# Two attention branches on one core: dense pieces that have no due date go into fewer and fuller slots

## The chip, the core and the metric

The kernel runs on one core of a Trainium2 chip. The metric is the device time in microseconds of one execution; three runs are given and their median is the time. Durations in the text come from one further execution that the hardware profiler recorded.

## The reference

Two attention branches over 2048 tokens of width 640 with 32 heads of 20, whose outputs stand side by side in the result. In short:

```python
# branch A: four segments of 512 tokens; q, k, v = x @ wq, wk, wv
for s in range(4):
    p = softmax(q[s] @ k[s].T * Dh**-0.5 + mask)      # mask falls on keys that come before the query
    a_mem = (phi(q[s]) @ M) / (phi(q[s]) @ z + 1e-6)    # phi(t) = t + 1 where t > 0, else exp(t)
    o[s] = g * a_mem + (1 - g) * (p @ v[s])             # g = sigmoid(beta), per head
    M = M + phi(k[s]).T @ v[s]; z = z + phi(k[s]).sum()
A = o @ wo
# branch B: q, k, v = x @ wqkv; causal window of 256 keys
B = softmax(where(0 <= i - j < 256, q @ k.T * Dh**-0.5, -1e9)) @ v @ wo
out = concatenate([A, B], axis=-1)
```

All arrays are bf16.

## The kernel before

The tokens are worked in four chunks of 512, and for each chunk the B branch and then the A branch: eight phases B0, A0, B1, A1, B2, A2, B3, A3. In a phase the 32 heads are eight groups of four (`Unit`). The scores of a group are cut into rectangles of key blocks and query blocks, and `Phase` puts them into packs of up to 512 query columns (`Pack`): 20 packs in a phase of A and in B0, 24 in the other phases of B, 172 in all.

Each pack is a **slot** of the loop in `body`, and slots are numbered through from 0 (B0 0 to 19, A0 20 to 39, B1 40 to 63, A1 64 to 83, B2 84 to 107, A2 108 to 127, B3 128 to 151, A3 152 to 171). The schedule is manual: what `body` records in this order is the order of each engine's queue. In one slot it does the following.

- It first runs what was put down for this slot (`self.after`): the spread of finished q or k from DRAM scratch into four row groups (L291, four DMAs on SP), and `normalise` (L544, L549 on DVE) of a group that was weighed four slots earlier (three in the last phase), which needs the transposed copy `ocT` that SP fetches by a DMA (L529).
- `scores` (L459) multiplies q and k on TensorE into two `Sc` tiles, one for two heads each. There are three such tiles in PSUM. ScalarE takes exp of each into `pt` (L465), and GpSimd clears what the masks exclude (L479, L485).
- It runs what was put down behind the scores (`self.behind`): for the memory of A, the phi of a projection made one and two slots before, an exp on ScalarE (L310) and steps on VectorE (L308, L313).
- Where a group's last pack lies two slots back, `weigh` (L514) multiplies its probabilities with v into a `D` tile; VectorE copies it (L527) and SP transposes it.
- Then come **dense pieces** that `pick` chooses: projections of q and k (`proj`, L267, copied at L270 and stored by L271), v for the coming chunk (`vproj`, L326, emptied at L332 or L334), and in A the memory's update (`upd`, L402) and read (`read`, L435, emptied by L442, L444 and L445), and halves of the output product (`out_half`, L580, emptied at L583, stored by L587).

Weighing and all dense pieces write PSUM tiles named `D`, of which there are two, so that a piece can start when VectorE has emptied the tile of the piece before the last one.

The planner of `body` has a cost for each piece in its own units: 1.19 for a projection, 0.79 for a v half, 0.75 for an output half and for a weighing, 0.4 for a read or an update, 0.45 for the scores. `total` is their sum over the phase, `part` the share of the phase's packs by weight that is done with this slot, and `room = total * part - done` is how far the phase lags behind an even spread. A piece may have a due slot; then `due` is what must be done now so that it isn't late, and where `due` is above `room` it takes its place and no output half is allowed. `pick` looks at the next three pieces of each kind and takes the combination whose cost comes nearest to `room`, with a term for the share of each kind that should be done by then.

Due dates stand on the pieces of B0, the first value and projection pieces of A0 and the first half of B1 (and on slot 13 of B1); the pieces of the later phases have none. What is left at a phase's end is done there, so that each phase has the same pieces in any case.

Of the kernel before, what the change touches and what calls it, by code (L numbers as in the profile page):

```python
# [82 lines left out]
class Kern:  # L83
# [572 lines left out]
    def body(self):  # L656
        phases = [Phase(br, c) for c in range(NC) for br in "BA"]
        lists, upd = self.plan()
        self.turned, self.half = [], []
        self.closing, self.open_masks = False, []  # L660
        for n, ph in enumerate(phases):
            dense = lists[n]
            mem = []
            if ph.br == "A" and ph.c > 0:
                mem = [(0.4, lambda tt=tt, hf=hf: self.read(ph.c, tt, hf))
                       for hf in range(2) for tt in range(CT)] + upd[ph.c]
            outs = 2 * OUT_TILES[n]
            np_ = len(ph.packs)
            weights = [pk.weight for pk in ph.packs]
            base = 0.45 * np_  # L670
            total = base + sum(a[0] for a in dense + mem) + 0.75 * outs + 0.75 * G
            done = 0.0
            at = [0, 0, 0]
            for i, pk in enumerate(ph.packs):
                while any(a[2] is not None and a[2] <= i for a in dense[at[0]:]):
                    done += dense[at[0]][0]
                    dense[at[0]][1]()
                    at[0] += 1
                for f in self.after.pop(self.slot, []):
                    f()  # L680
                last = n == len(phases) - 1 and i == np_ - 1
                if last:
                    self.last_turn("A", NC - 1, 0, 3)
                self.scores(pk, last)
                done += 0.45
                for f in self.behind.pop(self.slot, []):
                    f()
                if last:
                    break
                if self.ready and self.ready[0][0] <= self.slot:  # L690
                    self.weigh(self.ready.pop(0)[1])
                    done += 0.75
                self.prefetch()
                part = sum(weights[:i + 1]) / sum(weights)
                can = 2 * sum(1 for t in self.turned if t[0] + 2 <= self.slot) + len(self.half)
                room, ahead, due = total * part - done, 0.0, 0.0
                for a in dense[at[0]:]:
                    ahead += a[0]
                    if a[2] is not None:
                        due = max(due, ahead - 1.7 * (a[2] - 1 - i))  # L700
                if due > room:
                    room, can = due, 0
                for kind in self.pick(part, room, dense[at[0]:at[0] + 3],
                                      mem[at[1]:at[1] + 3], min(outs - at[2], can, 3),
                                      at, (len(dense), len(mem), outs)):
                    if kind == 2:
                        done += 0.75
                        self.out_step()
                    else:
                        a = (dense, mem)[kind][at[kind]]  # L710
                        done += a[0]
                        a[1]()
                    at[kind] += 1
                self.slot += 1
            for a in dense[at[0]:] + mem[at[1]:]:
                a[1]()
        self.tail("A", NC - 1)
# [101 lines left out]
```

## Time and profile before

| | us |
|---|---|
| median of 3 runs | 393.15 |
| lowest and highest run | 392.26, 395.36 |
| profiled execution | 390.19 |
| its span, from first to last instruction | 388.1 |
| TensorE matmul busy | 340.4 (88%) |
| ScalarE busy | 338.1 (87%) |
| VectorE busy | 276.7 (71%) |
| GpSimd busy | 251.8 (65%) |
| mean granted clock of TensorE | 0.991 of full speed |

PE in the profile is TensorE (matmuls; PEld is its weight load), ACT is ScalarE, DVE is VectorE, POOL is GpSimd and SP the engine that issues all DMAs of the kernel. Busy is the time in which an engine has at least one instruction in work. A row of the time order gives start, duration, engine, line, operation, tiles written and read, the number of instructions merged into it, and in square brackets how long the engine stood idle before it and who released it. A row of a stretch gives its bounds, its length, the busy time of each engine, the granted clock and the share of the DMA engines.

### The profile page before, as it was taken

How to read it: one execution, taken by the hardware profiler on the slowest of the kernel's cores; microseconds unless marked ns; L12 is line 12 of the kernel's file. 1: busy time of each engine (PE TensorE's matmuls, PEld its weight loads, DVE VectorE, ACT ScalarE, POOL GpSimd, SP SyncE). 2: the span in 40 equal slices, each digit the busy share in tenths (PEclk: the TensorE clock that was granted, in tenths of full speed). 3: DMA queues.
4: the chain of work that ended last, by engine and by line, in shares of the span. 5: the costliest groups of instructions: out<-in, count | busy, mean ns of one | idle time of the engine just before them, and what ended most of it. 6: DMA issues, size and time to landing. Idle time of an engine off the chain costs nothing.

```text
span 388.1 us, 10554 instructions
## 1 busy us (share of the span) xinstructions
PE 340.4 (88%) x4060; PEld 161.3 (42%) x4060; DVE 276.7 (71%) x581; ACT 338.1 (87%) x384; POOL 251.8 (65%) x392
## 2 busy tenths in 40 slices
PE   7999988977998798988997989898999989988884
PEld 3433434322443344444543335444454435544442
DVE  2467667634788868788778886789877887777583
ACT  2867789985999889888999999988999999999972
POOL 9657564542777587635578888844458988955550
PEclk9999999998999989999999999999999999999999
DMA  8993328647434597728575697758474377736312
GB/s 256 314 285 77 47 83 151 113 105 187 134 80 134 143 173 141 135 71 137 117 135 135 127 190 126 149 104 110 116 146 120 92 169 129 113 78 113 96 30 70
DMA packets 110738, 50.77 MB, mean 131 GB/s; under 512 B 81760, under 2 KB 110688, under 8 KB 110688
## 3 DMA queue, kind: packets, MB, share of 16 engines
q1 hardware_dynamic: 110688, 50.10, 61.1%
q8 instruction: 32, 0.52, 0.6%
q14 instruction: 18, 0.15, 0.1%
HBM read 16.39 MB, written 14.42 MB: 79 GB/s over the span
## 4 chain that ended last, share of the span: by engine, by line
PE 42%; ACT 24%; DVE 16%; issue 6%; POOL 6%; DMA 3%; SPq 0%; POOLq 0%; DVEq 0%; ACTq 0%
ACT pt L465 22%; PE D L267 13%; PE Sc L459 7%; PE D L326 6%; PE D L580 5%; PE D L514 5%; PE D L253 4%; POOL pt L479 3%; DVE qk L270 3%; POOL pt L485 3%; DVE oc L527 3%; ACT pe L310 2%; PE Sc L628 2%; DVE omem L445 1%; DMA ocT<-oc 1%
## 5 line engine op out<-in xcount | busy, mean ns | idle before, releaser
L465 ACT ACTIVATE pt<-Sc 128x1024 bf16<-128x1024 f32 (+1 forms) x344 | 320.7, 1077 | 32.3 <-PE Sc L459 28.2
L479 POOL TENSOR_SCALAR_AFFINE_SELECT pt<-pt 128x512 bf16<-128x512 bf16 x254 | 167.6, 671 | 117.2 <-ACT pt L465 116.9
L485 POOL TENSOR_SCALAR_AFFINE_SELECT pt<-pt 128x512 bf16<-128x512 bf16 x112 | 78.6, 717 | 5.1 <-ACT pt L465 4.8
L270 DVE CAST qk<-D 128x512 bf16<-128x512 f32 x70 | 47.9, 687 | 29.4 <-PE D L267 26.8
L527 DVE CAST oc<-D 128x512 bf16<-128x512 f32 x62 | 42.7, 688 | 19.9 <-PE D L514 19.8
L459 PE MATMUL Sc<-qpB,kpB 20*128 20x256 bf16 (+2 forms) x704 | 43.3, 277 | 7.8 <-ACT pt L465 4.7
L459 PE MATMUL Sc<-qpA,kpA 20*128 20x384 bf16 (+3 forms) x512 | 41.0, 302 | 5.8 <-ACT pt L465 5.0
L580 PEld LDWEIGHTS <-oT 128*128 128x128 bf16 x280 | 25.4, 98 | 17.9 <-issue 6.6
L583 DVE CAST ot<-D 128x320 bf16<-128x320 f32 x56 | 27.0, 485 | 7.2 <-PE D L580 6.4
L459 PEld LDWEIGHTS <-kpB 20*128 20x128 bf16 x704 | 13.6, 92 | 42.5 <-issue 38.5
L267 PE MATMUL D<-xTA,Aq 128*128 128x512 bf16 x100 | 24.9, 379 | 4.6 <-DVE oc L527 3.5
L326 PE MATMUL D<-Av,xTA 128*128 128x320 bf16 x160 | 26.2, 300 | 2.8 <-DVE vA L334 1.6
L514 PE MATMUL D<-pt,vA 128*32 128x256 bf16 (+3 forms) x576 | 23.5, 287 | 5.7 <-DVE qk L270 2.2
L580 PE MATMUL D<-Bo,oT 128*128 128x320 bf16 x160 | 27.3, 306 | 1.0 <-DVE omem L445 0.4
L267 PE MATMUL D<-xTA,Ak 128*128 128x512 bf16 x100 | 25.3, 384 | 2.1 <-DVE qk L270 2.0
L326 PE MATMUL D<-Bv,xTB 128*128 128x320 bf16 x160 | 26.0, 300 | 1.4 <-DVE oc L527 0.9
L514 PE MATMUL D<-pt,vB 128*32 128x384 bf16 (+2 forms) x720 | 26.1, 277 | 0.5 <-DVE qk L270 0.3
L459 PEld LDWEIGHTS <-kpA 20*128 20x128 bf16 x512 | 11.7, 91 | 30.6 <-issue 27.9
L267 PE MATMUL D<-xTB,Bq 128*128 128x512 bf16 x75 | 19.8, 396 | 3.4 <-DVE qk L270 3.2
L549 DVE TENSOR_TENSOR otB<-ocT,rr 128x320 bf16<-128x320 bf16 x32 | 20.2, 631 | 1.1
L544 DVE RECIPROCAL rr<-ocT 128x16 f32<-128x16 bf16 x62 | 15.1, 243 | 8.0 <-DMA ocT<-oc 8.0
L580 PE MATMUL D<-Ao,oT 128*128 128x320 bf16 x120 | 20.1, 299 | 0.7 <-DVE qk L270 0.4
(84 smaller groups left out, 358.8 us busy)
## 6 DMA issues: line engine op xcount, KB each, us to landing
out_dram<-ot SPq DMA_DIRECT2D x31, 160.0 KB
kdA<-qk SPq DMA_DIRECT2D x20, 128.0 KB
qdA<-qk SPq DMA_DIRECT2D x20, 128.0 KB
kdB<-qk SPq DMA_DIRECT2D x15, 128.0 KB
qdB<-qk SPq DMA_DIRECT2D x15, 128.0 KB
kpB<-kdB SPq DMA_DIRECT2D x8, 160.0 KB
qpB<-qdB SPq DMA_DIRECT2D x8, 160.0 KB
kpA<-kdA SPq DMA_DIRECT2D x8, 160.0 KB
```

The source lines that it names most:

```text
L267: nc.tensor.matmul(ps[:], lhsT=self.w[br + which][:, kt, m * P:(m + 1) * P], rhs=self.xT[br][:, kt, :], start=(kt == 0), stop=(kt == KT - 1))
L270: nc.vector.tensor_copy(out=t[:], in_=ps[:])
L326: nc.tensor.matmul(ps[:, 0:320], lhsT=self.xT[br][:, kt, tt * P:(tt + 1) * P], rhs=self.w[br + "v"][:, kt, hf * 320:(hf + 1) * 320], start ...
L459: nc.tensor.matmul(ps[j // 2][:, j % 2, off * P:(off + nq) * P], lhsT=kp[rows, u.g, k0:k0 + P], rhs=self.qp[u.br][rows, u.g, q0 * P:(q0 + ...
L465: nc.scalar.activation(out=pt[:, 2 * hp:2 * hp + 2, 0:pk.used], in_=ps[hp][:, :, 0:pk.used], func=ACT.Exp, scale=SCALE)
L479: nc.gpsimd.affine_select(out=blk, in_=blk, pattern=[[0, 4], [1, P]], compare_op=ALU.is_ge, fill=0.0, base=0, channel_multiplier=-1)
L485: nc.gpsimd.affine_select(out=blk, in_=blk, pattern=[[0, 4], [-1, P]], compare_op=ALU.is_ge, fill=0.0, base=-1, channel_multiplier=1)
L514: nc.tensor.matmul(O[32 * j:32 * j + 32, q0 * P:(q0 + nq) * P], lhsT=v[:, kt % CT, v0:v0 + 32], rhs=pt[:, j, off * P:(off + nq) * P], star ...
L527: nc.vector.tensor_copy(out=oc[:], in_=O[:])
L549: nc.vector.tensor_tensor(out=o[:, :, cols].rearrange("p b (j e) -> p b j e", j=4), in0=pv[:, :, :, 0:DH], in1=rr[:].unsqueeze(3).to_broad ...
L580: nc.tensor.matmul(ps[:, 0:320], lhsT=st["oT"][:, m, :], rhs=self.w[br + "o"][:, m, hf * 320:(hf + 1) * 320], start=(m == 0), stop=(m == K ...
L583: nc.vector.tensor_copy(out=st["ot"][:, hf * 320:(hf + 1) * 320], in_=ps[:, 0:320])
```

## The change

Where a slot's room is not set by a due date, and the slot is not the phase's last one, the room is set to nothing when it is under 0.9, and raised by 0.6 otherwise. The rest of the planner, the pieces, their order within each kind, and all instructions are as before.

```diff
                 if due > room:
                     room, can = due, 0
+                elif i < np_ - 1:
+                    room = 0.0 if room < 0.9 else room + 0.6
                 for kind in self.pick(part, room, dense[at[0]:at[0] + 3],
                                       mem[at[1]:at[1] + 3], min(outs - at[2], can, 3),
                                       at, (len(dense), len(mem), outs)):
```

## The prediction

> **What bounds the kernel now.** I read the engines' shares and the chain, then each phase's busy times, then single slots in time order.
>
> ```profile
> PE 340.4 (88%) x4060; PEld 161.3 (42%) x4060; DVE 276.7 (71%) x581; ACT 338.1 (87%) x384; POOL 251.8 (65%) x392
> ...
> PE 42%; ACT 24%; DVE 16%; issue 6%; POOL 6%; DMA 3%; SPq 0%; POOLq 0%; DVEq 0%; ACTq 0%
> ```
>
> PE and ACT are level, so averages settle nothing. The next rows are the phases A0, B1, A1, B2, A2, B3, A3, cut at the first score matmul of each (columns: stretch, its length, then each engine's busy us).
>
> ```profile
> 56.20:101.10 44.90, 37.98 (x376) 15.40 (x372) 25.53 (x50) 39.04 (x45) 21.93 (x34) 0.96 0.63 133
> 101.10:156.80 55.70, 49.68 (x575) 24.04 (x574) 43.97 (x90) 50.13 (x59) 41.01 (x63) 0.97 0.61 137
> 156.80:198.00 41.20, 37.25 (x449) 18.70 (x449) 32.27 (x79) 37.33 (x41) 21.75 (x34) 1.00 0.60 112
> 198.00:248.30 50.30, 43.93 (x535) 20.62 (x534) 41.17 (x78) 49.44 (x59) 42.47 (x63) 1.00 0.77 142
> 248.30:290.60 42.30, 38.86 (x458) 19.64 (x458) 33.89 (x80) 37.64 (x41) 22.07 (x34) 1.00 0.68 127
> 290.60:338.10 47.50, 45.25 (x541) 21.39 (x540) 36.69 (x70) 46.91 (x54) 41.81 (x63) 1.00 0.64 127
> 338.10:372.60 34.50, 29.58 (x375) 14.75 (x374) 25.53 (x63) 34.50 (x39) 20.82 (x33) 1.00 0.41 87
> ```
>
> B2, B3 and A3 are ACT's: it is idle 0.9, 0.6 and 0.0 us in them. A0, B1, A1 and A2 lose 4 to 6 us beyond ACT's work. All a better order can win from A0 to A3 is the sum of length minus ACT: 5.9 + 5.6 + 3.9 + 0.9 + 4.7 + 0.6 + 0.0 = 21.6 us, and PE must keep up for that: in A2 and B3 it is busy 38.9 of 42.3 and 45.3 of 47.5.
>
> The exp activations of a pack come in twos and run 14 in 12.94 us in an unbroken stretch from 187.77, so a pack costs ACT 1.85 us. In a slot PE does the scores (0.39), in two or three of five slots a weighing (0.66 alone), and the dense pieces: projection 1.19, value or output half 0.72, read 0.22, update 0.28 (all from unstalled slots). How far may PE run ahead? Slots 17 and 18 show it: 17 has no dense piece, 18 has two projections.
>
> ```profile
> 51.61 3.77 ACT L465 ACTIVATE pt<-Sc 128x1024 bf16<-128x1024 f32 x4 [1.35 <-POOL pt L485]
> 52.69 0.39 PE L459 MATMUL Sc<-qpB,kpB 20*128 20x384 bf16 x6 [1.03 <-ACT pt L465]
> ...
> 53.01 1.25 PE L267 MATMUL D<-xTA,Ak 128*128 128x512 bf16 x5
> ...
> 54.10 1.24 PE L267 MATMUL D<-xTA,Aq 128*128 128x512 bf16 x5
> ...
> 55.28 0.34 PE L459 MATMUL Sc<-qpB,kpB 20*128 20x384 bf16 x4
> ...
> 55.73 0.81 ACT L465 ACTIVATE pt<-Sc 128x768 bf16<-128x768 f32 x1 [0.35 <-PE Sc L459]
> ```
>
> After the empty slot PE stands 1.03 us before the second half of slot 18's scores, because the three Sc tiles are full; only when ACT frees one may it go on to the projections, and then ACT runs dry. From the first of four activations to the next pack's are 4.12 us for two packs of 1.85: 0.42 lost, behind an empty slot, with 2.38 us of dense work. So **a slot carries about 1.9 us of weighing and dense work free (2.38 - 0.42 = 1.96); what is above that is lost whole, however empty the slot before**. PE can't store the time of an empty slot: the Sc tiles hold a pack and a half.
>
> **The change part by part.** No instruction is added or removed on any engine. By the order of the two programs slots 0 to 27, ruled by due dates, stay, as does the tail; 113 of the slots from 28 on change. Of the 143 slots 28 to 170, 9 are without dense work before and 56 after, 37 of them with a weighing. The DMAs of moved pieces move with them; SP keeps its work.
>
> *1. Lumps.* I add up, over each slot, the us of weighing and dense work above 1.9. Before: 2.9 (slots 46, 48, 50 make 2.1 of it). After: A0 1.0 (3 slots), B1 3.8 (8), A1 4.1 (7), B2 4.7 (11), A2 3.7 (7), B3 4.3 (10), A3 0.5 (1), together 22.1. Typical: slot 103 (weighing, a value, two output halves: 2.82), 78 (2.82), 135 (weighing and two projections: 3.04). There is a credit: the 30 activations of L310 follow the scores of the slot after an A projection, mostly now an empty one, and give ACT 0.5 us each (two of them fill 130.28 to 131.32) while PE works at the fat slot. Where they stand before a fat slot they cover up to their length: 1.5 in B1, 3.1 in B2, 2.1 in B3, 6.7 in all, and 1.0 of the 2.9 before. Net 15.4 against 1.9: **+13.5**. In A3 alone PE has so much room (29.6 of 34.5) that lumps hardly matter. Bounds: a slot of a projection and an output half (1.91 us) behind a lean one cost nothing at 89 and 0.15 at 95 and 139, so the free amount could be up to 0.3 more, which by the same sum with slack carried from slot to slot makes +6; with no credit +19.
>
> *2. Waits for the two D tiles.* Every weighing and dense piece writes one and DVE empties it. In slot 68 (weighing and two reads) PE waits three times:
>
> ```profile
> 165.24 0.40 PE L459 MATMUL Sc<-qpA,kpA 20*128 20x384 bf16 x8
> 165.89 0.73 PE L514 MATMUL D<-pt,vA 128*32 128x512 bf16 x16 [0.26 <-DVE qk L270]
> 166.78 0.37 PE L435 MATMUL D<-mz,phiq 128*128 128x84 bf16 x5 [0.17 <-DVE omem L445]
> 167.41 0.36 PE L435 MATMUL D<-mz,phiq 128*128 128x84 bf16 x5 [0.25 <-DVE oc L527]
> ```
>
> A1 and A2 have 4.0 and 3.4 us of idle PE. Bare weighing slots lose these waits, but the reads then stand in threes behind a projection (slots 69, 113, 115): a read costs DVE 0.92 (165.75 to 166.67 in its order) against 0.22 on PE, so the second waits 0.7 and the third 0.9 more; twos of updates wait 0.4. I count 7.7 us of such waits in A1 and A2 against the 7.4 gone, of which some falls into slots under 1.9: -1 (bounds -7 and +4). In B1 to B3 about -1 likewise.
>
> *3. A0.* Slots 29 to 35 contain two DVE stops (2.74 and 3.31 us before L544) for late ocT transposes; SP is full there. The stops remain, since what stands before them in SP's queue is unchanged, but the empty slots 29, 31 and 34 let PE put scores ahead of blocked pieces: **-1.5** (bounds -4; +2, as the load of xTA and a store now stand ahead of slot 31's ocT).
>
> *4. PE's clock.* In slots 53 and 54, weighing alone and then nothing, PE is 2.12 of 3.5 us busy, and the next 3.4 us run at half clock:
>
> ```profile
> 133.70:137.20 3.50, 2.12 (x21) 0.77 (x21) 1.74 (x3) 3.50 (x5) 3.48 (x7) 0.99 0.83 168
> 137.20:140.60 3.40, 3.40 (x35) 1.43 (x37) 1.61 (x3) 2.22 (x3) 2.90 (x5) 0.50 0.98 148
> 365.00:368.40 3.40, 2.55 (x38) 1.23 (x36) 0.99 (x2) 3.40 (x5) 1.69 (x4) 1.00 0.28 71
> ```
>
> It made that projection 1.58 instead of 1.24, the output half 1.54 instead of 0.85, scores and weighing 0.6 longer: 1.6 us. With 2.55 of 3.4 it stayed at 1.00. A lean slot beside a fat one is like the last row; but 153, 156, 163 and 168 now start pairs of lean slots, all in A3, where PE has room. 0 to 4 x 1.6 = 6.4; I take **+1**. The Trainium skill ("TensorE: Matmul & The Clock Gate", Part 1: The HAM clock gate) states that the clock halves after an idle window of about 3.4 us; by that rule no pair would trip it and the sum would be 1 lower. The row at 137.20 disagrees: PE had not been idle a whole window.
>
> Sum: 13.5 - 1 - 1 - 1.5 + 1 = **+11 us**, against the profiled execution's 390.19 (span 388.1, 2.1 around it): 401. The median of the runs is 393.15, 1.0076 times the profiled one; so 404.
>
> **The rivals.** *Faster: the bare weighing slots free the D tiles.* All idle PE of A1 and A2 goes (-7.4), B1 to B3 save 2, A0 saves 4, and lumps cost only the +6 of the larger slack: -7.4, own time 383, median 386. For it: ACT starts each pack 0.5 us after its scores in nearly all of A1 and A2, so each PE wait there is paid. Against it: slot 18. It decides once the saved waits pass the lumps, a free amount of 2.2 us a slot. Chance 0.11.
>
> *Even: the two cancel.* Lumps +6, waits -2, A0 -1.5, clock 0 and a fat slot's own waits hidden: within 1% (about what a measurement of this kernel can tell from no change), 389.2 to 397.1; I put it at 395. Chance 0.13.
>
> *Slower by more: fat slots wait for DVE as well.* Two projections close together bring two L310 activations and four L308 and L313 operations at once; L313 already waits 7.2 us for L310 now, and DVE serves D in order, so a third piece in the slot waits. With no credit (+19), +4 in A1 and A2 and +4 in B2 and B3: own time near 415, median 418. Chance 0.15.
>
> *The clock falls at every lean slot.* 37 x 1.6 us is 59, a median near 453; the 365.00 row speaks against it: 0.02. The skill's same page (A second HAM failure mode: psum-queue depth-cycling) tells of a clock that oscillates as PE idles briefly between groups; no run here shows that so far.
>
> That the change does nothing is excluded by the order of the programs.
>
> **How the numbers follow.** Forecast (396 to 412) 0.59, slower by more 0.15 and clock 0.02: slower 0.76; even 0.13; faster 0.11. The range 389 to 419 goes from the lower edge of the even case to the end of the heavier one; 0.11 lies below and some 0.06 above.
>
> **What would show it.** Right: the same busy us of PE and ACT in work; ACT waits for PE Sc L459 well above the 28.2 us of now, in fat slots; PE Sc L459 waits for ACT grow past 9.7 in empty ones; B2 and B3 each 2 to 4 us longer, A1 and A2 2 to 3, A0 a little shorter, A3 about equal. Wrong: B2 and B3 as long as before (then the free amount is above 1.9 us), or A1 and A2 shorter (then bare weighing slots pay).

## The result, and the profile after

The changed kernel takes 429.68 us (median of 4 runs, 425.95 to 431.1) against 393.16: a ratio of 1.089, with a 95% interval from 1.080 to 1.098. The profiled execution took 428.49 us, its span is 426.5; the forecast for it was 401, and for the median 404, with a range to 419. The direction was right, and the loss is more than three times the forecast.

These are the lines of the page that answer to those of before, with the clock's row of the 40 slices:

```profile
PE 358.9 (84%) x4060; PEld 170.6 (40%) x4060; DVE 269.7 (63%) x581; ACT 340.8 (80%) x384; POOL 247.0 (58%) x392
...
PEclk9999989989999899999999889999999989868669
```

PE does the same 4060 matmuls and is busy 18.5 us longer, in a span 38.4 us longer: some of them ran slower. The clock's row shows where: at the end, with dips on the way. ACT's work has hardly grown; it waits. The list of waits has the two that the prediction named (us in total, times, longest):

```profile
ACT pt L465 <- PE Sc L459: 60.0, 58, 2.9
...
PE Sc L459 <- ACT pt L465: 31.3, 62, 1.3
```

Before they were:

```profile
ACT pt L465 <- PE Sc L459: 28.2, 36, 3.9
...
PE Sc L459 <- ACT pt L465: 9.7, 24, 1.0
```

The lumps thus do what was said of them: PE stands before full Sc tiles in the empty slots, ACT stands idle in the fat ones. The busy times by phase, A0 to A3, each cut again at its first score matmul:

```profile
58.30:102.20 43.90, 36.34 (x377) 15.32 (x375) 25.14 (x50) 39.49 (x45) 20.87 (x32) 0.96 0.61 135
102.20:159.60 57.40, 50.78 (x573) 24.45 (x573) 42.17 (x90) 49.90 (x59) 40.33 (x63) 0.97 0.53 129
159.60:204.80 45.20, 38.76 (x449) 19.47 (x449) 31.68 (x77) 37.42 (x40) 20.96 (x34) 1.00 0.53 107
204.80:263.50 58.70, 47.23 (x531) 22.43 (x530) 39.89 (x79) 50.25 (x60) 41.64 (x64) 0.94 0.59 121
263.50:309.60 46.10, 40.39 (x458) 20.56 (x458) 33.00 (x80) 38.06 (x42) 21.48 (x34) 1.00 0.60 118
309.60:363.00 53.40, 46.49 (x541) 22.83 (x540) 35.59 (x70) 47.31 (x54) 40.90 (x63) 0.97 0.50 113
363.00:409.50 46.50, 36.53 (x375) 17.23 (x374) 25.37 (x63) 36.03 (x39) 20.78 (x34) 0.77 0.27 65
```

A0 is 1.0 shorter; B1 is 1.7 longer, A1 4.0, B2 8.4, A2 3.8, B3 5.9 and A3 12.0, at a mean clock of 0.77. B0 is 2 longer and the tail 1.5, though neither changed: each has a stretch at half clock that the profiled execution before had not.

For the experiments I use two readings in all kernels. A phase's length goes from its first exp activation (L465) to that of the next phase (A3's to that of the last slot), and beside it stands how long the clock was granted at a half. A slot's **loss** is the time from its first exp activation to the next slot's, less 1.82 us, which is about this distance where ACT is never idle (the smallest is 1.81), and less 0.5 for each L310 activation in between.

### The profile page after: what moved, and what is told of

Its sections match the earlier page's. It is cut to its first block, busy times and chain, and to the rows that moved or that the text cites. A ratio compares the mean times of both kernels' runs of the same rounds, so it can differ in the third digit from the quotient of the medians.

```text
span 426.5 us, 10553 instructions
## 1 busy us (share of the span) xinstructions
PE 358.9 (84%) x4060; PEld 170.6 (40%) x4060; DVE 269.7 (63%) x581; ACT 340.8 (80%) x384; POOL 247.0 (58%) x392
## 4 chain that ended last, share of the span: by engine, by line
PE 51%; ACT 21%; DVE 14%; issue 6%; DMA 3%; POOL 2%; SPq 0%; ACTq 0%; DVEq 0%; POOLq 0%
ACT pt L465 19%; PE D L267 14%; PE Sc L459 10%; PE D L580 9%; PE D L326 7%; DVE qk L270 4%; PE D L514 4%; PE D L253 3%; DMA ocT<-oc 3%; ACT pe L310 2%; PE Sc L628 2%; POOL pt L485 1%; DVE oc L527 1%; DVE omem L445 1%; POOL pt L479 1%
## 5 line engine op out<-in xcount | busy, mean ns | idle before, releaser
L465 ACT ACTIVATE pt<-Sc 128x1024 bf16<-128x1024 f32 (+1 forms) x344 | 322.0, 1031 | 65.8 <-PE Sc L459 60.0
L479 POOL TENSOR_SCALAR_AFFINE_SELECT pt<-pt 128x512 bf16<-128x512 bf16 x254 | 165.9, 664 | 150.7 <-ACT pt L465 150.4
L485 POOL TENSOR_SCALAR_AFFINE_SELECT pt<-pt 128x512 bf16<-128x512 bf16 x112 | 75.5, 686 | 12.4 <-ACT pt L465 12.3
L459 PE MATMUL Sc<-qpB,kpB 20*128 20x256 bf16 (+2 forms) x704 | 45.8, 279 | 20.4 <-ACT pt L465 17.6
L459 PE MATMUL Sc<-qpA,kpA 20*128 20x384 bf16 (+3 forms) x512 | 44.1, 316 | 13.9 <-ACT pt L465 13.7
L580 PEld LDWEIGHTS <-oT 128*128 128x128 bf16 x280 | 28.5, 105 | 27.0 <-issue 11.4
L459 PEld LDWEIGHTS <-kpB 20*128 20x128 bf16 x704 | 14.6, 92 | 54.5 <-issue 50.4
L580 PE MATMUL D<-Bo,oT 128*128 128x320 bf16 x160 | 29.0, 323 | 4.6 <-DVE qk L270 2.0
L514 PE MATMUL D<-pt,vA 128*32 128x256 bf16 (+3 forms) x576 | 25.0, 302 | 6.0 <-DVE qk L270 4.3
L267 PE MATMUL D<-xTA,Aq 128*128 128x512 bf16 x100 | 26.4, 401 | 1.6 <-DVE oc L527 1.4
L580 PE MATMUL D<-Ao,oT 128*128 128x320 bf16 x120 | 23.4, 334 | 4.0 <-DVE oc L527 1.4
L514 PEld LDWEIGHTS <-vA 128*32 128x32 bf16 x576 | 12.9, 99 | 18.0 <-DVE qk L270 6.4
L334 DVE TENSOR_TENSOR vA<-D,omg 128x320 bf16<-128x320 f32 x32 | 15.5, 489 | 7.3 <-PE D L326 7.0
```

What stands on the lines that cost most here:

```text
L267: nc.tensor.matmul(ps[:], lhsT=self.w[br + which][:, kt, m * P:(m + 1) * P], rhs=self.xT[br][:, kt, :], start=(kt == 0), stop=(kt == KT - 1))
L334: nc.vector.tensor_tensor(out=self.v["A"][0][:, tt, hs, 0:DH], in0=src, in1=self.omg[:, hs].unsqueeze(2).to_broadcast([P, 16, DH]), op=ALU ...
L459: nc.tensor.matmul(ps[j // 2][:, j % 2, off * P:(off + nq) * P], lhsT=kp[rows, u.g, k0:k0 + P], rhs=self.qp[u.br][rows, u.g, q0 * P:(q0 + ...
L465: nc.scalar.activation(out=pt[:, 2 * hp:2 * hp + 2, 0:pk.used], in_=ps[hp][:, :, 0:pk.used], func=ACT.Exp, scale=SCALE)
L479: nc.gpsimd.affine_select(out=blk, in_=blk, pattern=[[0, 4], [1, P]], compare_op=ALU.is_ge, fill=0.0, base=0, channel_multiplier=-1)
L485: nc.gpsimd.affine_select(out=blk, in_=blk, pattern=[[0, 4], [-1, P]], compare_op=ALU.is_ge, fill=0.0, base=-1, channel_multiplier=1)
```

## The experiments

**1. The empty slots filled.** Unread matmuls (fillers) stand in the slots from A0 on that have neither a weighing nor a dense piece, and in slot 54:

```diff
+                if bare and n > 0 and (at == was or self.slot in WARM):   # bare: nothing weighed; WARM = (54,)
+                    self.warm()
...
+    def warm(self):
+        ps = self.dtile([P, CH], F32)
+        w = self.w["Bo"]
+        for i in range(4):
+            self.nc.tensor.matmul(ps[:], lhsT=w[:, 0, 0:P], rhs=w[:, 0, 0:CH], start=True, stop=True)
```

> The changed kernel, with four matmuls of 512 columns whose result nobody reads put at the end of each slot that has neither a weighing nor a dense piece (18 slots), and of slot 54; about 0.9 us of PE each, where PE otherwise waits for a Sc tile. Clock theory: PE's low activity in empty slots lets the granted clock fall to a half, and the half clock lengthens the next dense work; with the gaps filled the falls in A3 go, A3 (46.5 us) comes back to 35 to 37, B2 and B3 lose 2 each, and the profiled time falls from 428.5 to 410 to 414. Rival, lumps: A3 loses by its fat slots alone and the clock is a by-product; the added matmuls take PE time, A3 stays above 44 and the time is 427 to 432.

Measured: 416.82 us, a ratio of 1.059 [1.051, 1.067], 12.9 less by adding work. The time lies between the two theories: B2 became 2.8 us shorter and B3 0.8, as the clock theory had it, but A3 stopped at 41.5, with 3.4 us of half clock left in it where there were 22.2. So 5 to 6 us of A3's 12 were the clock's (experiment 4 has A3 without any half clock), and some 6 are something else.

**2. The last phase planned as before.**

```diff
-                elif i < np_ - 1:
+                elif i < np_ - 1 and n < 7:
                     room = 0.0 if room < 0.9 else room + 0.6
```

> The changed kernel, but the last phase (A3) planned as before; phases B0 to B3 are as changed. If A3's share of the loss is all made in A3, the span falls by A3's 12.0 us and by what the tail lost (1.5): about 415 of 428.5. If the phase only pays for what earlier phases put off (DVE or DMA work that is late), A3 stays over 38 and the time is 420 or more.

Measured: 416.74 us, 1.064 [1.056, 1.071]; profiled 414.93. A3 is 34.6 us, as in the kernel before, and the tail 14.9. A3's loss is made in A3; nothing was put off into it.

**3. L313 behind the weighing.** `rest` of `phi`, which waits for an exp on ACT, is recorded one step later in the slot:

```diff
-        self.at_end(self.slot + 2, rest)
+        self.late.setdefault(self.slot + 2, []).append(rest)
...
                 if self.ready and self.ready[0][0] <= self.slot:
                     self.weigh(self.ready.pop(0)[1])
                     done += 0.75
+                for f in self.late.pop(self.slot, []):
+                    f()
                 self.prefetch()
```

> The changed kernel, with the last step of phi (L313 on DVE) recorded behind the weighing of its slot instead of ahead of it, so that the copy of the weighed tile (L527) doesn't stand behind it in DVE's queue; nothing else. DVE theory: in slots 91, 97 and 141 a third piece waits 1.0 to 1.4 us for the copy, which stands behind two L313 that wait for exps on ACT; these waits shrink, and B2 and B3 together lose 3 to 4 us: 424 to 426. Rival: PE's own lumps set these slots, the time stays within 1 us of 428.5.

Measured: 421.54 us, 1.071 [1.065, 1.077]; 8 less (424 to 426 was expected), of which part is that this program's runs had less half clock (by the runs' mean clocks 39 us in the median run, 52 in the changed kernel's). At equal clock the slots answer: 91 lost 2.23 and loses 0.93, 97 went from 1.61 to nothing, 141 from 0.98 to nothing, 3.9 in all. Slot 50, a weighing and two projections, goes from 1.52 to 0.01 too, but it loses the same 1.52 in the kernel before: that part of the gain undoes nothing of the change. This is slot 97 of the changed kernel in time order:

```profile
236.25 0.84 PE L514 MATMUL D<-pt,vB 128*32 128x384 bf16 x24 [0.44 <-DVE qk L270]
236.29 1.23 ACT L310 ACTIVATE pe<-qk 128x512 bf16<-128x512 bf16 x2
...
237.76 1.18 DVE L313 TENSOR_TENSOR phiq<-phiq,pe 128x512 bf16<-128x512 bf16 x2
...
238.86 0.68 DVE L527 CAST oc<-D 128x512 bf16<-128x512 f32 x1
...
239.59 0.84 PE L326 MATMUL D<-Av,xTA 128*128 128x320 bf16 x5 [1.31 <-DVE oc L527]
...
240.85 1.02 ACT L465 ACTIVATE pt<-Sc 128x1024 bf16<-128x1024 f32 x1 [1.51 <-PE Sc L459]
```

The weighing is done at 237.1, but its copy starts at 238.86, behind two L313 that had waited for two exps; the value piece needs that D tile and stands 1.31 us. The same slot with the order changed and the empty slots filled (experiment 4; the lines are numbered one higher):

```profile
233.80 0.84 PE L515 MATMUL D<-pt,vB 128*32 128x384 bf16 x24
...
234.69 0.69 DVE L528 CAST oc<-D 128x512 bf16<-128x512 f32 x1 [0.82 <-PE D L515]
...
235.30 1.12 DVE L314 TENSOR_TENSOR phiq<-phiq,pe 128x512 bf16<-128x512 bf16 x2
...
236.93 1.94 ACT L466 ACTIVATE pt<-Sc 128x1024 bf16<-128x1024 f32 x2 [0.20 <-PE Sc L460]
```

The copy follows the weighing at once, and ACT waits 0.20 instead of 1.51.

**4. Both edits (1 and 3).**

> The changed kernel with both earlier edits: unread matmuls in its empty slots, and L313 behind the weighing. If clock and DVE's order are two causes, they add: 416.8 less the 2 us of B2 and 1 of B3 that the second edit gave, 411 to 415; slots 91, 97 and 141 as in the run with L313 moved, and at least half of the half-clock time of A3 gone. If the second edit helped by the clock only, it gives nothing more here: 416 to 418.

Measured: 414.34 us, 1.062 [1.055, 1.069]; profiled 413.18. They add: 2.5 less than with the filler alone, and slots 91, 97 and 141 together lose 1.4 instead of 4.0. One slot is worse: 64 loses 1.94 where the changed kernel loses 1.10, since its projection waits 0.79 us for VectorE to empty a value's tile. A3 can be seen at full clock here: no half clock at all, and still 40.3 us where the kernel before takes 34.6.

**5. Fillers behind the weighings too.** Edits 1 and 3, and the filler in every slot without dense work:

```diff
-                if bare and n > 0 and (at == was or self.slot in WARM):
-                    self.warm()
+                if at == was or self.slot in WARM:
+                    self.warm(4 if bare else 3)
```

(`warm` takes the number of matmuls here.)

> The changed kernel with L313 behind the weighing, and unread matmuls in every slot without dense work, those with a weighing too (three of them there, four elsewhere). Clock theory: what the half clock still cost (some 13 us of it, at 0.35 to 0.6 us each) goes but for the fall behind the DVE stop in A0: 407 to 411, with the granted clock at 0.99. What is left against the kernel before, 15 us and more, is then the lumps and waits for D. Rival, no more than a filler's cost: 413 or above, as the matmuls behind the weighings delay the scores.

Measured: 425.79 us, 1.082 [1.074, 1.090]. The profiled execution had 0.996 of the clock and yet took 421.81, 8.6 more than that of experiment 4: A1 49.1 instead of 47.6, A2 48.6 instead of 45.9, A0 45.7 instead of 42.9. The rival holds. In slot 64 the projection waits 1.12 us for D, in most fat slots of A2 0.2 more is lost, and slots of a weighing alone, which lost nothing, lose 0.2 to 0.5 (112, 117, 119). A full clock isn't worth that.

**6. Shorter work of DVE behind a read.** In both kernels one copy takes the place of L442, L444 and L445; the division by z and the gate are left out:

```diff
-        nc.vector.scalar_tensor_tensor(out=rr[:], in0=pv[:, :, DH], ...)
-        nc.vector.reciprocal(out=rr[:], in_=rr[:])
-        nc.vector.tensor_tensor(out=self.omem[...], in0=pv[:, :, 0:DH], in1=rr[...], op=ALU.mult)
+        nc.vector.tensor_copy(out=self.omem[...], in_=pv[:, :, 0:DH])
```

> The changed kernel, with the memory's read emptied by one copy instead of L442, L444 and L445: the memory branch's division by z and its gate are left out, so a read keeps its D tile for about 0.5 us of DVE instead of 0.92. Waits-for-D theory: in fat slots with reads (64, 69, 73, 108, 113, 115 in A1 and A2; 152, 155, 158, 160, 165 in A3) the piece behind a read waits for DVE, so each of them loses about 0.45 us less per such wait: A1 and A2 together 2 to 3 less, A3 2 to 4 less at equal clock. Rival, PE's own work sets these slots: they stay within 0.1 us each.

> The same cut (division by z and gate of the memory's read left out) in the kernel before, as control. There reads stand in pairs behind a weighing and lose 0.54 to 0.65 us a slot in 65, 68 and 114; waits-for-D theory: these shrink to 0.1 to 0.3, A1 and A2 together 1 to 2 us less, A3 the same as ACT sets it. Rival: no change.

Measured: 416.98 and 393.11 us, one run each, with 28 and 21 us of half clock, so that the totals can't be compared with others; the slots can. Losses of slots in us; those with L442 to L445 are from experiment 4, so that A3's are at full clock too, except 64, which is from the changed kernel; the blank is a slot whose clock was halved:

| slot | pieces | with L442 to L445 | one copy |
|---|---|---|---|
| 69 | PBk r r r | 1.51 | 0.99 |
| 113 | PBk r r O | 1.97 | 1.45 |
| 115 | PBq r r r | 1.51 | 0.99 |
| 64, 108 | PBk r O | 1.10 | 1.10 |
| 152 | r r O | 0.64 | 0.04 |
| 155 | r O O O | 1.29 | 0.73 |
| 158 | weighing, r r O | 1.58 | 0.98 |
| 160 | r O O | 0.56 | none |
| 165 | r r O O | 1.54 | |

(PBk and PBq are projections of k and q for B, r a read, O an output half.) Where a piece waits for a read, 0.5 to 0.6 goes, and A3 gains 2.3 in the four slots; A1 and A2 gain 1.6 there, less than expected, since in slots 64, 73 and 108 the last piece waits for the projection's copy and not for the read's. In the control the pairs of reads behind a weighing kept their loss (65, 68 and 114 at 0.65, 0.54 and 0.54): that part of the expectation fell; the slots behind such pairs gained (66, 70 and 73: 0.3 to 0.5 each), and A1 was 1.3 shorter. Slot 115 of the changed kernel:

```profile
281.73 0.36 PE L435 MATMUL D<-mz,phiq 128*128 128x84 bf16 x5
...
282.67 0.36 PE L435 MATMUL D<-mz,phiq 128*128 128x84 bf16 x5 [0.58 <-DVE qk L270]
...
283.57 0.38 PE L435 MATMUL D<-mz,phiq 128*128 128x84 bf16 x5 [0.54 <-DVE omem L445]
...
283.88 0.40 PE L459 MATMUL Sc<-qpA,kpA 20*128 20x512 bf16 x4
```

Three reads of some 0.2 us on PE take 2.2 us, from 281.73 to 283.88, because each must wait for DVE to empty the D tile of the piece before the last.

**7. Two Sc tiles in the kernel before.**

```diff
-        ps = [self.ps.tile([P, 2, CH], F32, name="Sc", bufs=3) for _ in range(2)]
+        ps = [self.ps.tile([P, 2, CH], F32, name="Sc", bufs=2) for _ in range(2)]
```

> The kernel before with two Sc tiles in place of three (the tail's third tile has a name and place of its own). Theory that the Sc tiles set the free amount: with two, PE can start a pack's second half only when ACT has ended the whole pack before, so about 1.0 us of weighing and dense work a slot is free instead of 1.9; over the slots of before the excess grows from about 9 to 77 us, of which phi's activations cover some 10 and PE's own bound in B0 some more: 430 to 455. Rival, that ACT's idle time comes from VectorE and D alone: under 400.

Measured: 448.24 us, one run. That lies within the 430 to 455 of the theory and far from its rival's "under 400", but the slots show another mechanism than the theory's, so that the hit is luck:

```profile
226.01 1.94 ACT L465 ACTIVATE pt<-Sc 128x1024 bf16<-128x1024 f32 x2
...
228.00 0.39 PE L459 MATMUL Sc<-qpB,kpB 20*128 20x384 bf16 x6 [0.56 <-ACT pt L465]
...
228.47 1.94 ACT L465 ACTIVATE pt<-Sc 128x1024 bf16<-128x1024 f32 x2 [0.52 <-PE Sc L459]
```

`scores` records both tiles for a pack's first rectangle before either for its second. So with two tiles six of the eight matmuls of a pack of two rectangles, among them two for its first tile, wait until ACT has ended the whole pack before (226.01 + 1.94), and ACT waits for them in turn, however little dense work there is. Of 75 slots from 40 on, at full clock, without L310 and with such a pack next, 68 lose 0.57 to 0.66 us, those with 0.7 us of weighing and dense work (101, 105, 148, 153, 163: 0.59 to 0.64) like those with 1.9 (89, 95, 118: 0.62). By the theory the former would have lost nothing. Ahead of a pack of one rectangle most slots with up to 1.5 us lose next to nothing (110, 122, 125: 0.00). The run shows that the third tile is worth much, not that the free amount falls to 1.0; part of the 55 us is also that 36 us of this execution ran at half clock.

**8. The kernel before with fillers**, in its two slots that have neither weighing nor dense work (the edit of experiment 1):

> The kernel before, with the same unread matmuls in its two slots without weighing and dense work, 54 and 170. Clock theory: the half clock at 137.2 to 140.6 goes, which cost 1.2 to 1.6 us there; 0.996 to 0.997 of the time before, the fall behind the DVE stop at 89.4 stays. Rival: the fall has nothing to do with the lean slots 53 and 54, and the ratio is 1.000 within 0.001.

Measured: 392.33 us, 0.999 [0.996, 1.002]: not told apart from no change. The fall near 137 is gone (B1 54.5 instead of 55.7), but others stand near 53 and 214 that the profiled execution before hadn't. Experiment 9, without a filler, has no fall near 137 either, so it isn't shown that the filler removed it.

**9. The kernel before, with the change in A0 alone and L313 behind the weighing.**

```diff
                     room, can = due, 0
+                elif n == 1 and i < np_ - 1:
+                    room = 0.0 if room < 0.9 else room + 0.6
```

> The kernel before, with the change in phase A0 alone and with L313 behind the weighing. A0 gained 1.1 us by the change, and the copy of a weighed tile can only come earlier: A0 42.5 to 43 instead of 44, the rest within 0.5: ratio 0.995 to 0.998. Rival: A0's gain was one of the clock's falls, which come by chance; then 1.000 within 0.002.

Measured: 392.11 us, 0.999 [0.994, 1.004]: undecided; A0 43.4, between the 42.5 to 43 expected and the 44.0 of before.

**10. All that helped, on the kernel before**: experiment 9 with fillers in the slots without weighing and dense work, slots 17 and 54 among them.

> The kernel before with the change in A0 alone, L313 behind the weighing, and unread matmuls in the empty slots 17, 54 and in any other slot that has neither weighing nor dense work. If the falls near 50 and 135 come from those lean slots they go, 1.5 us each where they occur, on top of 1 us from the other two edits: ratio 0.990 to 0.995. If falls come by chance and only change places: 0.998 to 1.000.

Measured: 390.34 us, 0.9945 [0.991, 0.998]. It is a little faster than the kernel before, at the edge of what was expected. Which edit did it isn't shown: B0 is 46.0, without the fall that experiments 8 and 9 had there, but the profiled execution before had none there either (46.5), and slot 50 lost nothing instead of 1.52, as in experiment 9.

## Why the prediction was wrong

Three steps of the sum failed: step 4 above all (the clock), step 1 (its free amount and its credit) and step 2 (which left out the D tiles of A3).

**The lumps (step 1, +13.5) were rightly seen, but the free amount was too large.** Slots of projections lost about what was forecast with 1.9 us free: slot 66, two projections, 0.53 (0.48 forecast), 110 0.73 (0.70), 118 0.78 (0.76). That emptiness can't be stored held too: slot 55, behind two lean slots, loses 0.54 to 0.57 at full clock, no less than 66 behind one. But slots of values and output halves lost more: 105 and 125 (three of them) 0.48 and 0.47 for 0.26, 78 1.24 and 103 1.36 for 0.92, 76 and 120 1.10 and 1.08 for 0.73. With 60 and 148 (0.51 and 0.56 for 0.26) these eight slots lost 6.8 us where 4.3 was forecast. Slot 105 shows which term was wrong:

```profile
257.95 1.53 PE L326 MATMUL D<-Av,xTA 128*128 128x320 bf16 x10
...
259.39 0.84 PE L580 MATMUL D<-Bo,oT 128*128 128x320 bf16 x5
...
260.16 0.40 PE L459 MATMUL Sc<-qpB,kpB 20*128 20x384 bf16 x8
```

The three pieces take 2.21 us, from 257.95 to 260.16, hardly more than the 2.16 forecast, and 0.48 of it is lost: 1.73 was free. The same count, from a slot's first piece to the next scores less the loss, gives 1.71 to 1.75 in 66, 69, 78, 103, 108, 110, 115, 118, 120 and 125, whatever the pieces. The forecast took 1.9 from slot 18 by counting two projections as 2.38 us; its own rows have them in 2.27 (53.01 to 55.28). So the term mis-sized is the free amount, and that slots of two projections came out right is luck: both numbers were too large by nearly the same. An estimate with 1.73 free and 1.13 for a projection gives 22.7 us of net lumps ahead of the credit instead of 19.2, 3.5 more.

**The credit inside step 1 (6.7 us) failed where it mattered.** It held for two projections behind a lean slot (89, 95 and 139 lost 0.05 or less). In 91, 97 and 141, which carry a weighing, it was to cover everything, and they lost 4.8 us together. The activation of L310 does give ACT work, but its partner L313 waits for it on DVE and holds the weighed tile's copy: the 2.57 us of work in such a slot took 3.8 to 4.8. Experiments 3 and 4 show this: the order alone takes 2.6 (with fillers) to 3.9 us out of these three slots. The prediction had this as its rival, slower by more; the place was right.

**Step 2 (waits for D) was right in A1 and A2 and left A3 out.** As forecast, the bare weighing slots lost nothing any more: 65, 68, 70, 75, 109, 112, 114, 117, 119 and 124 lost 6.8 us in the kernel before. And the fat slots took as much again: with the lumps, A1 and A2 were to be 6.6 us longer (4.1 + 3.7 - 0.2 - 1), and are 7.8. But the same count was not made for A3, where reads and output halves are all there is; since PE is only busy 29.6 of 34.5 us there, I took it for safe. Mean room doesn't help a fat slot: at full clock A3 is 5.7 us longer (experiment 4), 5.6 of it in the five slots 152, 155, 158, 160 and 165, and shorter DVE work per read takes back 2.3 in four of them (experiment 6).

**Step 3 (A0, -1.5 and 1.0 of lumps) came out about right**: A0 is 1.0 shorter. In the experiments that keep the changed A0 without fillers behind weighings it was 42.5 to 44.0 us, against 44.0 before; experiment 9 could not resolve it in the whole.

**Step 4 (the clock, +1) is the largest miss: about 13.** In the profiled execution 49 us were granted at a half, against 7. Over 51 runs of the kernel before, which differ in mean clock from 0.960 to 0.996, time rises 0.36 us for each us at half clock, with a correlation of 0.93; 42 x 0.36 is an estimate of 15 us, and experiment 1 took 12.9 off directly, with some half clock left. I had counted four pairs of lean slots, at most 6.4 us, and trusted that a window of 75% activity is safe; and I had left out that a fall can last. These rows are consecutive windows of A3 in the changed kernel:

```profile
374.40:377.80 3.40, 2.10 (x32) 0.72 (x32) 1.34 (x3) 3.34 (x4) 1.22 (x2) 1.00 0.33 87
377.80:381.20 3.40, 2.57 (x33) 1.53 (x30) 2.10 (x7) 2.27 (x3) 1.64 (x3) 0.50 0.55 110
381.20:384.60 3.40, 2.63 (x19) 0.81 (x18) 1.39 (x4) 1.76 (x2) 0.22 (x1) 0.50 0.12 25
384.60:388.00 3.40, 3.40 (x23) 1.52 (x21) 1.72 (x5) 2.02 (x3) 1.85 (x3) 0.50 0.08 29
388.00:391.40 3.40, 3.20 (x46) 1.58 (x38) 2.17 (x6) 3.13 (x4) 1.06 (x2) 1.00 0.25 60
```

PE is busy 2.10 of 3.40, and the clock halves. In the next two windows it is busy 2.57 and 2.63, even with matmuls that take twice as long, and stays at a half; after one that is full it comes back. With fillers the same phase ran at 1.00 (experiment 4). The Trainium skill ("TensorE: Matmul & The Clock Gate", Part 1: The HAM clock gate) has the clock halve after an idle window of about 3.4 us; by that rule none of these would have fallen, and the rows disagree. Its section "A second HAM failure mode: psum-queue depth-cycling", a clock that oscillates with short idle times of PE, comes nearer to these rows; I gave it 0.02, with a price of a fall at every lean slot. The truth lay between: 14 windows at half clock.

The misses add up: clock 12, credit and DVE's order 5, A3's waits 5, the free amount 3.5; that is some 25 of the 27.5 us between 401 and 428.5, and the rest is not assigned. They overlap a little, since the fillers also took 0.6 from slot 97. The last figure is an estimate from single slots and was not tried by an experiment. Which single windows fall in a given run was not settled: B0, which the kernels before and after have alike, had a fall near 53 in one profiled execution and not in the other.

## What to carry to other kernels

Between two engines that are both near full, the tiles between them are the store of time: work out from the time order, with the durations that stand there and not with rounded costs, how much uneven work a step carries free (here 1.73 us with three tiles), and don't let a planner make lumps above it, since the empty steps gave nothing back here. Check a theory like this in single slots: the total of experiment 7 fitted one that its slots contradict. Count the waits for the other shared tiles in every phase, also in those with room on average. And look at the clock's windows before leaving gaps on PE: filling a gap with useless matmuls brought 12.9 us here, yet the same filler one place further cost 11.

## What was not expected of the hardware

In the profiled executions of the two kernels and of experiments 1, 2, 3 and 8, every window of 3.41 us after which the clock halved had PE matmuls busy for 2.32 us or less, and every one with 2.35 or more kept it; below, both occurred (1.68 of 3.41 once stayed). Of 38 windows at half clock the seven with 2.14 to 2.83 us of PE were followed by another, the 31 with 3.16 and more by full clock. Neither is a rule: in experiment 7 the clock halved after a window with 2.58 us of PE (from 390.0), and stayed at a half after windows with 3.41 and 3.20 (from 393.4 and 396.8). What decides besides PE's busy time is open.

All falls of one execution lie on one grid of 3.41 us (91.1 - 53.5 is 11.0 of them, 241.2 - 138.8 is 30.0), in all 13 profiled executions. That would let the same gap fall in one run and not in another, and so explain much of the spread of the runs of the kernel before, 388.3 to 397.9, which goes with their time at half clock; that the grid's place decides it is not shown.
